# Where transform sets stand between the matmuls of a gated MLP

## The chip, the cores and the metric

The kernel runs on one core of a Trainium2 chip. The time is device microseconds (us) from one launch; lower is better. A core has engines that run side by side, each through its own list of instructions in order: TensorE (PE, matmuls, writes to PSUM), VectorE (DVE), ScalarE (ACT), GpSimd (POOL) and SyncE (SP), which here issues nearly all DMA transfers. They wait for each other by semaphores.

## The reference, cut to what matters

Two blocks are applied to the same layer-normed input, their results are added, and the gradients with respect to nine inputs are computed as well. S = 2048 rows, D = 512 columns, F = 1376 hidden columns, all bfloat16.

```python
xn  = layernorm(x)
kv  = shift_conv(k, shift_k) * v                  # 4 taps along the rows
y   = irfft(rfft(kv, 2S) * rfft(ssm_k, 2S))[:S] + kv * ssm_D
A   = xn * y                                      # long convolution
B   = ((xn @ w_gate) * (xn @ w_up)) @ w_down      # gated MLP
out = x + A + B
# and the vector-Jacobian product of out with grad_out
```

The backward pass needs a second convolution (of grad_out * xn, for dkv) and a third correlation (for d ssm_k), and for the MLP the gradient of its hidden layer, dx and three weight gradients.

## The kernel before, in words

The long convolution is a transform in two steps. `stage1` multiplies each of 16 blocks of rows by a table and stores the result in DRAM (FD), one for each of three signals. Eight groups (`groups`, L710) then do the second step: for group g and signal sg, `g_fwd` (L554) loads a tile X from FD and does sixteen matmuls that use a 64 by 32 part of the array (ps, two PSUM tiles); ScalarE copies both to SP (S1). `g_mul` (L569) multiplies two such spectra on VectorE: two long products T and U (L577), then an addition or subtraction for each half of T (L579, L580). `g_inv` (L583) does sixteen matmuls on T into two PSUM tiles (pg), ScalarE copies them to GO, and SP stores GO in DRAM (GD). Sixteen such matmuls, forward or inverse, are called a **set** here. There are 24 forward and 24 inverse ones. A forward set also issues the load of the X that is four further on (L567).

The MLP goes through eight chunks of 256 rows. `ffn1` (L478) does a chunk in six **pieces** of two hidden blocks (the sixth has one): gate and up (pgu, sixteen matmuls of 256 columns), the gradient of the hidden layer (pdh, eight), copies on ScalarE (gu, dh), products on VectorE (hd), a store of hd (HDD). `yb` (L518) follows one chunk behind: for each of two halves of the rows (sb), y (py, eleven matmuls of 512 columns; VectorE adds x, L529) and dx (px, twenty-two matmuls over two weights; ScalarE copies it, L535).

Both are Python generators. `main` (L748) yields after every piece of `ffn1` and after every y and dx of `yb`. The loop at L770 adds a pace to an account at every such yield and moves a second generator, `side`, one step for every whole number in the account. `side` is first `front` (the normalisation and `stage1`, at 170/71 steps per yield), then `groups`, which sets the pace to GPACE = 0.96. `groups` issues four loads of X, then yields four times with nothing in between, then goes through its sets, one per step (before the first inverse set is one more empty step). So about every piece, y and dx is followed by a set. In what order the instructions stand on each engine in the end is decided by the layer that records them, which has priorities (`high_priority` lifts copies and products) and its own estimates.

PSUM has three tiles of two banks (P2: pgu, ps, pg, later pt, pq, pu) and two of one bank (P1: pdh, py, px, later pd). ps and pg take two of the three.

Behind the stage stands a tail (`dw` and its sides, L911 and L1063): 2048-column transposes of hd out of HDD (tile hb, transposes pt, copies nath and natd), weight gradients (pd, pu), the last transform step (`st1p`, pq, on tiles g1 that are loaded from GD, L793), and elementwise work. Its first loads (hb, g1) are issued behind the last store of GD on SP. These names are used below.

Of the kernel before, what the change touches and what calls it, by code (L numbers as in the profile page):

```python
# [25 lines left out]
NCH = 8  # L26
# [150 lines left out]
def kernel(  # L177
# [42 lines left out]
    def act(o, i):  # L220
        nc.scalar.copy(o, i)  # L221
# [16 lines left out]
    def P2(name, shape, dt=F32):  # L238
        return ps2.tile(shape, dt, name=name, tag="p2")

    def P1(name, shape, dt=F32):
        return ps1.tile(shape, dt, name=name, tag="p1")
# [235 lines left out]
    def ffn1(ch):  # L478
        xt, gt = XT.pop(ch)
        hd = hds[ch % 2]  # L480
        HD[ch] = hd
        for fb0 in range(0, NFB, 2):
            blk = FBLK[fb0:fb0 + 2]
            n = len(blk)
            fw = blk[0][1]
            pgu = P2("pgu", [P, 2, 2, 256])
            pdh = P1("pdh", [P, 2, 256])

            def gate_up():
                for i, (f0, w) in enumerate(blk):  # L490
                    for t, W in enumerate((Wu, Wg)):
                        for c in range(NC4):
                            nc.tensor.matmul(pgu[:w, i, t, :], lhsT=W[:, c, f0:f0 + w], rhs=xt[:, :, c, :],  # L493
                                             start=(c == 0), stop=(c == NC4 - 1))

            def down():
                for i, (f0, w) in enumerate(blk):
                    for c in range(NC4):
                        nc.tensor.matmul(pdh[:w, i, :], lhsT=WdT[:, c, f0:f0 + w], rhs=gt[:, :, c, :],  # L499
                                         start=(c == 0), stop=(c == NC4 - 1))  # L500

            for f in ((gate_up, down) if ch or fb0 else (down, gate_up)):
                f()
            if ch == 0:
                mid(fb0 // 2)
            gu = gup.tile([P, 2, 2, 256], BF, name="gu")
            dh = gup.tile([P, 2, 256], BF, name="dh")
            act(gu[:fw, :n], pgu[:fw, :n])
            act(dh[:fw, :n], pdh[:fw, :n])
            with tc.high_priority(offset=SOON):  # L510
                nc.vector.tensor_tensor(hd[:fw, fb0:fb0 + n, 0, :], gu[:fw, :n, 0, :], gu[:fw, :n, 1, :], op=ALU.mult)  # L511
                nc.vector.tensor_tensor(hd[:fw, fb0:fb0 + n, 1:3, :], gu[:fw, :n],  # L512
                                        dh[:fw, :n].unsqueeze(2).to_broadcast((fw, n, 2, 256)), op=ALU.mult)
            if ch < NCH - 1:
                nc.sync.dma_start(HDD[:, fb0:fb0 + n, ch], hd[:, fb0:fb0 + n])
            yield

    def yb(ch):  # L518
        hd = HD.pop(ch)
        bx = ybo.tile([P, 2, 2, D], BF, name="bx")  # L520
        xb = ybo.tile([P, 2, D], BF, name="xb", bufs=1)
        nc.sync.dma_start(xb[:], x_n[:, 2 * ch:2 * ch + 2, :])
        for sb in range(2):
            ss = slice(sb * 128, (sb + 1) * 128)
            py = P1("py", [P, D])
            for fb, (f0, fw) in enumerate(FBLK):
                nc.tensor.matmul(py[:], lhsT=hd[:fw, fb, 0, ss], rhs=Wd[:fw, fb, :], start=(fb == 0), stop=(fb == NFB - 1))  # L527
            with tc.high_priority(offset=SOON):
                nc.vector.tensor_tensor(bx[:, sb, 0, :], py[:], xb[:, sb, :], op=ALU.add)  # L529
            yield  # L530
            px = P1("px", [P, D])
            for t, W in ((1, WTS[0][:, 0]), (2, WTS[0][:, 1])):
                for fb, (f0, fw) in enumerate(FBLK):
                    nc.tensor.matmul(px[:], lhsT=hd[:fw, fb, t, ss], rhs=W[:fw, fb, :], start=(t == 1 and fb == 0), stop=(t == 2 and fb == NFB - 1))  # L534
            act(bx[:, sb, 1, :], px[:])  # L535
            if sb == 1:
                nc.sync.dma_start(BX[:, 2 * ch:2 * ch + 2, :, :], bx[:])
            yield

# [5 lines left out]
    def g_load(n):  # L547
        g, sg = divmod(n, 3)
        if g < 8:
            X = gpool["x"].tile([P, 4, D], BF, name="X", bufs=4)  # L550
            nc.sync.dma_start(X[:], FD[sg, 16 * g:16 * g + 16].rearrange("k c r d -> (k c r) d").rearrange("(q m) d -> m q d", q=4))
            GX[n] = X

    def g_fwd(g, sg):  # L554
        X = GX.pop(3 * g + sg)
        S1 = gpool["a"].tile([P, 2, 2, D], BF, name="SP", bufs=4)
        for ri in range(2):
            ps = P2("ps", [P, 2, D])
            for q in range(4):
                for a in range(2):  # L560
                    nc.tensor.matmul(ps[32 * q:32 * q + 32, a, :],  # L561
                                     lhsT=TB.EF[64 * a:64 * a + 64, 4 * g + q, ri].rearrange("p k j -> p (k j)"),
                                     rhs=X[64 * a:64 * a + 64, q, :], start=True, stop=True)
            with tc.high_priority(offset=SOON):
                act(S1[:, ri], ps[:])
        GS[sg] = S1
        g_load(3 * g + sg + 4)  # L567
# [37 lines left out]
    def seq(*its):  # L605
        for it in its:
            for _ in it:
                yield
# [40 lines left out]
    def mid(n):  # L649

        if n == 0:
            wd_transposes(*WPARTS[1])
        elif n == 2:
            wd_transposes(*WPARTS[2])
# [55 lines left out]
    def groups():  # L710
        st_es.close()
        gpool["a"] = gpool["es"].enter_context(tc.tile_pool(name="ga", bufs=1, side="right", reuse_waits="tile"))
        gpool["x"] = gpool["es"].enter_context(tc.tile_pool(name="gx", bufs=1, side="right", reuse_waits="tile"))
        for n in (0, 2, 3, 1):
            g_load(n)
        pace[0] = GPACE
        for _ in range(4):
            yield
        g_fwd(0, 0)
        yield  # L720
        g_fwd(0, 2)
        g_mul(1, 0, 2, True)
        yield
        g_fwd(0, 1)
        g_mul(0, 0, 1, False)
        g_mul(2, 1, 2, True)
        yield
        yield
        g_inv(0, 0)
        yield  # L730
        for g in range(1, 9):
            for sg, dg, o, ops in ((0, -1, 1, ()), (1, -1, 2, ((0, 0, 1, False),)),
                                   (2, 0, 0, ((1, 0, 2, True), (2, 1, 2, True)))):
                if g < 8:
                    g_fwd(g, sg)
                    for m in ops:
                        g_mul(*m)
                    yield
                if g + dg < 8:
                    g_inv(g + dg, o)  # L740
                    yield

    GPACE = 0.96
    pace = [170 / 71]
    gpool["es"] = ExitStack()
    side = seq(front(), groups())

    def main():  # L748
        for ch in range(NCH):
            it = ffn1(ch)  # L750
            for n, _ in enumerate(it):
                if ch == 0:
                    tables(n)
                yield
                if n == 1 and 0 < ch < NCH - 1:
                    load_xt(ch + 1)
                if ch == 0 and n == 3:
                    load_xt(1)
                if n == (5 if ch == 1 else 1) and 0 < ch < NCH - 1:
                    while len(WTS) < 2:  # L760
                        next(side)
                    yield from yb(ch - 1)
        yield "wa"
        yield from yb(NCH - 2)
        yield from yb(NCH - 1)

    mainit = main()
    acc = -5 * pace[0]
    mdone = 0
    for tag in mainit:  # L770
        if tag == "wa":
            wa_es.close()
            c1 = ctx.enter_context(tc.tile_pool(name="c1", bufs=1, reuse_waits="tile"))
            xnC = c1.tile([P, R, D], BF, name="xnC")
            goC = c1.tile([P, R, D], BF, name="goC")
            nc.sync.dma_start(goC[:], go_n)
            nc.sync.dma_start(xnC[:], XN[:])
        acc += pace[0]
        while acc >= 1:
            acc -= 1  # L780
            next(side, None)
    for _ in side:
# [319 lines left out]
```

## Time and profile before

| | |
|---|---|
| time, median of 3 runs | 508.24 us (505.66 to 508.82) |
| profiled execution, its own time | 507.66 us |
| its span, first to last instruction | 505.9 us |
| busy: TensorE, VectorE, ScalarE | 479.2, 341.0, 328.7 us |
| mean granted clock of TensorE | 0.996 |
| 131.6 us to 153.2: TensorE busy | 21.50 of 21.60 us |
| 153.2 us to 325.0: TensorE, ScalarE busy | 168.57, 126.67 of 171.80 us |
| 325.0 us to 337.0: TensorE busy | 11.71 of 12.00 us |

The transform sets begin at 137 us and end at 313 us; dx of the last chunk ends at 325 us and the tail begins. In lines of the trace in order of time, the columns are start, length, engine, line, operation, tiles (out<-in), shapes and the number of instructions that are merged into the line; brackets tell how long the engine was idle before it and what ended that. In a list of waits the numbers are the total, the number of times and the longest. "Issue" as what was waited for means that the profile shows nothing.

### The profile page before, as it was taken

The numbers are of one execution on the slowest core, as the hardware profiler recorded it, in microseconds if no ns is written. First come the engines' busy times: TensorE is split into PE (matmuls) and PEld (weight loads), VectorE is DVE, ScalarE is ACT, GpSimd is POOL, SyncE is SP. The second block draws the span as 40 slices with busy tenths as digits, with TensorE's granted clock in tenths as the row PEclk, the third lists the DMA queues.
The fourth block names the chain that finished last, engine by engine and source line by source line (L and its number), as shares of the span: only waits on it lengthen the run. The fifth ranks groups of instructions, "written<-read, shape, count | busy, mean of one in ns | idle before, by whom it ended". The sixth has DMA issues, their size and how long they took to land.

```text
span 505.9 us, 10724 instructions
## 1 busy us (share of the span) xinstructions
PE 479.2 (95%) x4420; PEld 323.4 (64%) x4457; DVE 341.0 (67%) x633; ACT 328.7 (65%) x358; POOL 6.7 (1%) x17
## 2 busy tenths in 40 slices
PE   8789889998999999999999999999999989999996
PEld 7677554645747547547457733566776768777885
DVE  3987998888365748866648956031288987999800
ACT  3676788857837949759569975286575524555551
POOL 3000000000000000000000000020000000000000
PEclk9998999999999999999999999999999999999999
DMA  9999997989896957967968396999999999897513
GB/s 279 375 330 335 292 298 250 341 269 344 299 296 212 278 187 242 289 206 233 271 198 264 127 343 222 374 359 370 375 334 342 371 294 351 269 309 240 166 60 108
DMA packets 98045, 140.41 MB, mean 278 GB/s; under 512 B 18474, under 2 KB 72047, under 8 KB 96108
## 3 DMA queue, kind: packets, MB, share of 16 engines
q1 hardware_dynamic: 96668, 138.94, 83.3%
q10 hardware_dynamic: 1328, 0.79, 0.5%
q8 instruction: 35, 0.57, 0.5%
q14 instruction: 14, 0.11, 0.1%
HBM read 72.76 MB, written 63.41 MB: 269 GB/s over the span
## 4 chain that ended last, share of the span: by engine, by line
PE 55%; DMA 20%; DVE 10%; ACT 9%; issue 3%; SPq 2%; ACTq 0%
PE px L534 12%; PE pgu L493 9%; PE pu L939 8%; PE py L527 6%; PE pdh L499 5%; PE pd L922 4%; DMA FD<-fst 3%; PE pg L590 2%; PE pt L815 2%; PE ps L561 2%; ACT gu L221 2%; DMA out_dram<-o 2%; DMA khC<-in_A_k_dram 2%; DMA bb<-BX 2%; ACT fst L221 2%
## 5 line engine op out<-in xcount | busy, mean ns | idle before, releaser
L939 PE MATMUL pu<-natd,xnC 128*128 128x256 bf16 (+1 forms) x704 | 79.1, 270 | 0.7 <-ACT nath L221 0.7
L534 PE MATMUL px<-WT,hd 128*128 128x512 bf16 (+1 forms) x346 | 78.9, 379 | 0.5 <-issue 0.3
L939 PEld LDWEIGHTS <-xnC 128*128 128x128 bf16 x704 | 67.2, 98 | 8.7 <-issue 1.0
L534 PEld LDWEIGHTS <-hd 128*128 128x128 bf16 (+1 forms) x352 | 33.5, 98 | 42.7 <-issue 3.7
L221 ACT COPY natd<-pt 128x2048 bf16<-128x2048 bf16 (+1 forms) x22 | 40.4, 1838 | 25.4 <-PE pt L815 25.4
L493 PE MATMUL pgu<-xt,Wu 128*128 128x256 bf16 (+1 forms) x352 | 53.3, 274 | 3.5 <-DVE WdT L224 2.0
L493 PE MATMUL pgu<-xt,Wg 128*128 128x256 bf16 (+1 forms) x352 | 52.8, 273 | 0.0
L221 ACT CAST gu<-pgu 128x1024 bf16<-128x1024 f32 (+1 forms) x48 | 45.3, 946 | 11.3 <-PE pgu L493 11.0
L221 ACT CAST GO<-pg 128x1024 bf16<-128x1024 f32 x48 | 46.3, 1019 | 7.7 <-issue 4.8
L577 DVE TENSOR_TENSOR T<-SP 128x2048 bf16<-128x2048 bf16 x24 | 29.3, 1223 | 31.9 <-ACT SP L221 31.9
L499 PE MATMUL pdh<-gt,WdT 128*128 128x256 bf16 (+1 forms) x352 | 47.1, 275 | 1.5 <-DVE WdT L224 1.3
L221 ACT CAST SP<-ps 128x1024 bf16<-128x1024 f32 x48 | 46.6, 1034 | 1.9 <-PE ps L561 1.9
L221 ACT CAST fst<-pf 128x1024 bf16<-128x1024 f32 x40 | 39.2, 1034 | 12.5 <-DMA FD<-fst 10.8
L493 PEld LDWEIGHTS <-Wu 128*128 128x128 bf16 (+1 forms) x352 | 33.0, 100 | 19.9 <-issue 15.1
L527 PE MATMUL py<-Wd,hd 128*128 128x512 bf16 (+1 forms) x166 | 40.5, 380 | 0.8 <-issue 0.5
L499 PEld LDWEIGHTS <-WdT 128*128 128x128 bf16 (+1 forms) x352 | 34.9, 101 | 6.8 <-DVE WdT L224 1.5
L922 PE MATMUL pd<-goC,nath 128*128 128x512 bf16 (+1 forms) x166 | 38.3, 379 | 0.5
L221 ACT CAST bx<-px 128x512 bf16<-128x512 f32 x16 | 9.5, 592 | 45.1 <-PE px L534 45.1
L493 PEld LDWEIGHTS <-Wg 128*128 128x128 bf16 (+1 forms) x352 | 34.9, 100 | 3.6
L511 DVE TENSOR_TENSOR hd<-gu 128x512 bf16<-128x512 bf16 (+1 forms) x48 | 19.1, 398 | 24.3 <-ACT gu L221 24.2
L512 DVE TENSOR_TENSOR hd<-gu,dh 128x1024 bf16<-128x1024 bf16 (+1 forms) x48 | 30.7, 642 | 1.1 <-ACT dh L221 0.2
L527 PEld LDWEIGHTS <-hd 128*128 128x128 bf16 (+1 forms) x176 | 16.3, 98 | 22.8 <-issue 4.8
(155 smaller groups left out, 677.7 us busy)
## 6 DMA issues: line engine op xcount, KB each, us to landing
HDD<-hd SPq DMA_DIRECT2D x35, 384.0 KB, 4.8
hb<-HDD SPq DMA_DIRECT2D x10, 1344.0 KB, 11.4
FD<-fst SPq DMA_DIRECT2D x24, 512.0 KB, 3.9
X<-FD SPq DMA_DIRECT2D x24, 512.0 KB, 5.5
GD<-GO SPq DMA_DIRECT2D x24, 512.0 KB, 3.8
g<-GD SPq DMA_DIRECT2D x8, 1024.0 KB, 8.8
BX<-bx SPq DMA_DIRECT2D x8, 512.0 KB, 3.4
bb<-BX SPq DMA_DIRECT2D x8, 512.0 KB, 7.6
```

The costliest lines, as they stand in the source:

```text
L221: nc.scalar.copy(o, i)
L493: nc.tensor.matmul(pgu[:w, i, t, :], lhsT=W[:, c, f0:f0 + w], rhs=xt[:, :, c, :], start=(c == 0), stop=(c == NC4 - 1))
L499: nc.tensor.matmul(pdh[:w, i, :], lhsT=WdT[:, c, f0:f0 + w], rhs=gt[:, :, c, :], start=(c == 0), stop=(c == NC4 - 1))
L511: nc.vector.tensor_tensor(hd[:fw, fb0:fb0 + n, 0, :], gu[:fw, :n, 0, :], gu[:fw, :n, 1, :], op=ALU.mult)
L512: nc.vector.tensor_tensor(hd[:fw, fb0:fb0 + n, 1:3, :], gu[:fw, :n], dh[:fw, :n].unsqueeze(2).to_broadcast((fw, n, 2, 256)), op=ALU.mult)
L527: nc.tensor.matmul(py[:], lhsT=hd[:fw, fb, 0, ss], rhs=Wd[:fw, fb, :], start=(fb == 0), stop=(fb == NFB - 1))
L534: nc.tensor.matmul(px[:], lhsT=hd[:fw, fb, t, ss], rhs=W[:fw, fb, :], start=(t == 1 and fb == 0), stop=(t == 2 and fb == NFB - 1))
L561: nc.tensor.matmul(ps[32 * q:32 * q + 32, a, :], lhsT=TB.EF[64 * a:64 * a + 64, 4 * g + q, ri].rearrange("p k j -> p (k j)"), rhs=X[64 * a ...
L577: tt(W[:].rearrange("p c a d -> p c (a d)"), A[:, i:i + 1].rearrange("p c a d -> p c (a d)").to_broadcast((P, 2, 2 * D)), B[:].rearrange(" ...
L590: nc.tensor.matmul(pg[q // 2][64 * a:64 * a + 64, q % 2, :], lhsT=TB.EI[32 * q:32 * q + 32, 2 * g + a, yi].rearrange("p k c -> p (k c)"), ...
L922: nc.tensor.matmul(pd[:fw, :], lhsT=nt[:, r, :fw], rhs=goC[:, r, :], start=(r == 0), stop=(r == R - 1))
L939: nc.tensor.matmul(pu[:, c, :, :fw], lhsT=xnC[:, r, cs(c)], rhs=ng[:, :, r, :fw], start=(r == 0), stop=(r == R - 1))
```

## The change

The pace is replaced by named places as soon as `groups` has begun. Each yield of `main` now carries a value; where it is true, `side` moves one step. It is true behind every y and every dx, behind the first half of every dx (a new yield between the two weights, `"half"`), and behind the first, third and fifth piece of a chunk; in the last chunk behind all pieces but the sixth. While `front` runs the pace is as it was, and `"half"` doesn't count. The four empty steps at the start of `groups` become one.

```diff
 def ffn1(ch):
-            yield
+            yield fb0 in (0, 4, 8) or (ch == NCH - 1 and n > 1)
 def yb(ch):
                 nc.vector.tensor_tensor(bx[:, sb, 0, :], py[:], xb[:, sb, :], op=ALU.add)
-            yield
+            yield True
             px = P1("px", [P, D])
             for t, W in ((1, WTS[0][:, 0]), (2, WTS[0][:, 1])):
                 for fb, (f0, fw) in enumerate(FBLK):
                     nc.tensor.matmul(px[:], lhsT=hd[:fw, fb, t, ss], rhs=W[:fw, fb, :], start=(t == 1 and fb == 0), stop=(t == 2 and fb == NFB - 1))
+                if t == 1:
+                    yield "half"
             act(bx[:, sb, 1, :], px[:])
...
-            yield
+            yield True
 def groups():
         for n in (0, 2, 3, 1):
             g_load(n)
-        pace[0] = GPACE
-        for _ in range(4):
-            yield
+        pace[0] = None
+        yield
         g_fwd(0, 0)
...
-    GPACE = 0.96
 def main():
-            for n, _ in enumerate(it):
+            for n, set_here in enumerate(it):
...
-                yield
+                yield set_here
...
-        acc += pace[0]
-        while acc >= 1:
+        if pace[0] is None:
+            if tag and tag != "wa":
+                next(side, None)
+            continue
+        if tag != "half":
+            acc += pace[0]
+        while acc >= 1 and pace[0]:
             acc -= 1
             next(side, None)
```

A chunk's pieces and its `yb` thus hold nine places (three and six) where the pace gave 9.6 steps (5.76 and 3.84). The built program has the same instructions as before in another order. On TensorE the order is the same up to the first transform set and, but for a matmul here and there, from the first pu on.

## The prediction, made before the run

> **What bounds the kernel now.** I read the page's busy shares first, then TensorE's list of waits in the stage that changes (137 us, the first transform matmul, to 325 us, the last matmul of dx), then the same stretch in order of time.
>
> ```profile
> PE 479.2 (95%) x4420; PEld 323.4 (64%) x4457; DVE 341.0 (67%) x633; ACT 328.7 (65%) x358; POOL 6.7 (1%) x17
> ```
>
> TensorE is the bound. Its waits between 137 and 325 us (total, times, longest):
>
> ```profile
> PE ps L561 <- ACT GO L221: 1.5, 4, 0.7
> PE py L527 <- issue: 0.5, 3, 0.2
> PE pg L590 <- ACT SP L221: 0.5, 2, 0.2
> PE px L534 <- issue: 0.3, 2, 0.2
> ```
>
> The two "issue" rows are no waits: in each such place the first matmul of the chain has no record (x10 or x21 where the code has 11 or 22). What is left is 2.0 us of 188, all of it TensorE waiting for ScalarE to empty a PSUM buffer, where a set follows the sixth MLP piece of a chunk. By the distance of its starts (281.34 to 284.62) ScalarE needs 0.93 + 0.48 us for a piece (gu, dh) and 1.87 for a set, 3.28; TensorE needs 2.61 for the piece (pgu at 131.63 to the next at 134.24) and 0.67 for the set, also 3.28. From 260 to 293 us ScalarE is busy 32.97 of 33.00 us. So **no more than 2.0 us can be gained in the stage itself**, and all else depends on its two ends, where now TensorE does not wait:
>
> ```profile
> 142.43 1.23 DVE L577 TENSOR_TENSOR T<-SP 128x2048 bf16<-128x2048 bf16 x1 [1.64 <-ACT SP L221]
> ...
> 147.96 1.22 DVE L577 TENSOR_TENSOR T<-SP 128x2048 bf16<-128x2048 bf16 x1 [1.84 <-ACT SP L221]
> 149.11 1.22 DVE L577 TENSOR_TENSOR U<-SP 128x2048 bf16<-128x2048 bf16 x1
> 150.24 0.68 DVE L529 TENSOR_TENSOR bx<-py,xb 128x512 bf16<-128x512 f32 x1
> 150.84 0.68 DVE L579 TENSOR_TENSOR T<-T,U 128x1024 bf16<-128x1024 bf16 x1
> 151.44 0.68 DVE L580 TENSOR_TENSOR T<-T,U 128x1024 bf16<-128x1024 bf16 x1
> ```
>
> The first product ready for an inverse set is done at 152.1; the set starts at 153.20, 1.1 us later. The other end:
>
> ```profile
> 312.53 0.64 PE L590 MATMUL pg<-T,EI 32*64 32x512 bf16 x16
> 315.65 0.46 SPq L799 DMA_DIRECT2D hb<-HDD  x1
> 316.21 1.63 SPq L793 DMA_DIRECT2D g<-GD  x2
> 325.00 0.94 PE L815 MATMUL pt<-ident,hb 128*128 128x128 bf16 x14
> 325.89 1.89 PE L837 MATMUL pq<-g,IW 128*128 128x512 bf16 x8
> 326.10 1.86 ACT L221 COPY nath<-pt 128x2048 bf16<-128x2048 bf16 x1 [0.31 <-PE pt L815]
> 336.94 3.76 PE L939 MATMUL pu<-natd,xnC 128*128 128x256 bf16 x33
> ```
>
> The last set ends at 313.1; its copies free SP at 315.6, SP then issues the loads of hb (6.9 us to landing, at 322.5) and g (8.9 and 9.9, at about 325.1 and 326.6), and dx and y of the last chunk (11.9 us) cover both.
>
> **The change part by part.** No engine gets or loses work; the built order has 49 entries into a group of transform matmuls before and 49 after (28 of them behind an MLP piece before, 17 after). An entry costs TensorE about 0.10 us wherever it stands (pdh at 155.53 to ps at 156.50: 0.97 for eight matmuls at 0.109; px at 183.61 to ps at 188.47: 4.86 for 22 at 0.217). So the move itself is worth nothing, and splitting px for a set costs nothing more.
>
> 1. *Sets beside y and half dx.* A set every 11 matmuls of 0.217 us plus 0.67 is one in 3.05 us, against 1.9 us of ScalarE (and 0.58 for bx twice a chunk); in the MLP a set on every second piece is 3.28 + 1.41 = 4.7 us of ScalarE against 5.9 of TensorE. I followed the three PSUM buffers through a chunk by hand with these durations and found no wait. On SP each set's X load and GD store move with it; they change places with neighbouring stores and with the two transposing loads of a chunk (3.2 and 4.0 us of SP's time). An X lands in 5.5 us and is used four forward sets after its issue, some 24 us in the densest part; a GO buffer comes round after three inverse sets, 18 us there, against 3.8 us for its store. That cover is ample. **-2.0 us**; if ScalarE's start is late (chunk 7 keeps sets on five pieces in a row) -1.0.
>
> 2. *One empty step in place of four at the start.* The first forward set stands one MLP piece earlier, so it is reached at 134.24 instead of 136.96. Its X was issued at 129.85 and took 4.8 us: 134.65. With the 0.05 until TensorE starts: **+0.45** (0 to 1.85, had it taken the 6.2 us of the next but one). The second forward set then comes after the same work as before, at 140.45 (before 139.99). The third comes after half of dx, 143.5, not all of it plus a wait (145.41); its X is the one that waits for the last FD write, issued at 137.3, and lands by 143.5 at 6.2 us: nothing.
>
> 3. *The first inverse set.* VectorE's chain starts 0.46 later than in the rows above, at 142.9, runs the first product to 146.5 and then, in the built order, T, U, one more T of the third product (1.14 apart), the add that makes half of the second product's T (done 150.6), bx, the other add (done 151.8). TensorE has after the third set half of dx, y, three matmuls of dx: it is at the first eight matmuls of the inverse set at 149.6 and waits to 150.65, is at the second eight at 151.25 and waits to 151.85. **+1.65** (0.9 if the T of the third product slips behind, 2.6 if bx and that T both delay it). The cover that hid this, half of dx more, is what the change takes away.
>
> 4. *The last products.* Behind the last forward set (at k) ScalarE and VectorE need as before 2.56 us until the first T starts, then 1.14 + 1.14 + 1.14 to the add: half of T at k + 6.65, all at k + 7.25. The inverse set that reads it was 8.5 us behind (301.01 to 309.48); now two half-chains are in between, 0.57 + 2.38 + 0.10 twice, k + 6.1. Waits 0.55 and 0.35: **+0.9** (0 to 1.6). The last product is done at k + 10.3 and its second eight matmuls are due at k + 10.4: nothing.
>
> 5. *The junction.* Behind the last set now stand half of dx, y, dx: 44 matmuls, 9.6 us, not 55. hb is issued 2.55 us after the set's end and lands after 6.9, at 9.45: just in time (up to +1 if it takes longer). g lands 2.4 to 3.4 us after the end of dx (call it P). The built order has taken this into account: behind the first 16 transposes comes one matmul of pd, which needs their copy (nath, 1.86 us), and only then pq. In before pq filled that gap. So TensorE waits from P + 1.05 to P + 3.05; then pq to 5.0, two groups of transposes to 7.1, 15 of pd to 10.4, pq to 12.2, transposes; ScalarE copies yC from 4.3 to 6.25, natd twice to 9.95, od, dd to 13.25, and the PSUM buffer of that dd is the one for pu: pu at P + 14.2, before P + 11.95: **+2.25** (lower end +0.7: the later wait of 1.55 us of pk for khC, at the end of a chain through SP and VectorE, may swallow 1.55). And SP now has the store of the last bx, which waits for the end of dx, ahead of the second g load: issued at P + 1.2, not 8 us before P; at 8.9 to 11.0 us it lands at P + 10.1 to 12.2, for a pq due at P + 10.4: **+0.7** (0 to 1.8). Behind it on SP hb, v and k loads start 0.5 us later.
>
> Behind that the order of the tail is the same, and TensorE is 95% busy there, so nothing gives the delay back.
>
> **Sum:** 0.45 + 1.65 - 2.0 + 0.9 + 2.25 + 0.7 = +3.95. The profiled execution took 507.66 us (span 505.9), 0.58 below the median 508.24: 507.66 + 3.95 = **511.6 us**. Lower ends together: 0 + 0.9 - 2.0 + 0 + 0.7 + 0 = -0.4, 507.3; upper ends: 1.85 + 2.6 - 1.0 + 1.6 + 2.25 + 1.8 + 1 = +10.1, 517.8.
>
> **Rivals.**
> *ScalarE's relief alone counts.* Place: the sixth piece of each chunk, price -2.0 us: 505.7. It decides once the two ends together cost under 2.0 us: it needs VectorE's first and last chain 1 us faster each, and g early enough that the scheduled pd matmul is the only wait, given back at khC. For it: the chain that ended last runs from the end of dx through SP's loads, VectorE and khC to pk, and TensorE has slack of 1.55 there. Against: that chain itself starts with the same products and copies. Chance 0.25, 504.5 to 509.
>
> *Loads at the junction take the busy time.* hb loads elsewhere take 10.5 us in the median and up to 11.9, the third g took 11.0. If hb takes 10.5 now that 2.4 us of cover is gone: +3.6 in front of everything, with the rest 515.2; the second g at 11 adds 1. Chance 0.2, 513.5 to 518.
>
> *It does not do what it says.* The recording layer still orders by its own estimates: it put three matmuls of dx before the first inverse set and split that. Elsewhere the built order has the sets where named. If the sets' places do not matter to any wait: 507.7. Chance 0.05.
>
> *TensorE's clock.* Granted clock is 1.00 in the changed stage and 0.99 over the first 131.6 us, where TensorE's longest wait is 2.2: 1.3 us is all that a start from rest has cost. The waits above are at most 2.0 each; if one of them grew and lost the clock, +1.3: 512.9. Chance 0.02, inside the forecast's range. The Trainium skill (TensorE: Matmul & The Clock Gate, Part 1: The HAM clock gate) puts the loss of clock behind an idle window of about 3.4 us; by it these waits lose none. The trace agrees so far: waits up to 0.70 in the stage, clock 1.00.
>
> **Chances.** Forecast (+2 to +6 us, 509.7 to 513.7) 0.48, relief 0.25, slow loads 0.2, no effect 0.05, clock 0.02. 1% is 5.1 us, about what a measurement tells from no change, so 503.2 to 513.3 is "within". Forecast but its top, relief, no effect: 0.66; slower by more: 0.31; faster by more would need more than the 2.0 us that exist: 0.03. Range 506 to 516.
>
> **What would show it.** Right: TensorE's waits for ScalarE's GO and SP in the stage go to about 0; a wait of 1 to 2.6 us of the first pg for T around 150 us, one of about 1 us around the last group, pd waiting about 2 us for nath at the end of dx, pu starting 14 us behind it. Wrong: pg without a wait for T, hb landing clearly after dx ends, or pq waiting for g by 2 us and more; a shift that comes from the MLP chunks in between would mean that I misjudged ScalarE.

## The result, and the profile after

| | before | after |
|---|---|---|
| time, median (13 runs each) | 507.23 us (505.53 to 508.82) | 509.64 us (508.42 to 512.16) |
| profiled execution, its own time | 507.66 us | 509.33 us |
| its span | 505.9 us | 507.5 us |
| mean granted clock of TensorE in it | 0.996 | 0.992 |

The ratio of the times is **1.0061, with a 95% interval of 1.0043 to 1.008**: some 3.1 us slower (2.2 to 4.1), inside 1%. The forecast was +3.95 us and the range 506 to 516.

To place the loss, both traces are cut at three matmuls that stand at the same point of the work: the first pgu of chunk 2 (call it A; the order of TensorE is the same up to there), the first pt of the tail (P, the end of dx) and the first pu of the tail.

| us | start to A | A to P | P to pu | pu to end |
|---|---|---|---|---|
| before | 131.63 | 193.37 | 11.94 | 168.96 |
| after | 132.02 | 192.93 | 15.18 | 167.37 |
| difference | +0.39 | -0.44 | +3.24 | -1.59 |

The first column is no effect of the change: the point A lies between 131.1 and 133.9 us in all the traces of this study, with the same order in front of it. The second column, the stage that the change is about, comes out 0.4 us shorter; the third, twelve microseconds at the end of dx, loses 3.2. These two executions are only 1.6 us apart, because the last column gives 1.59 back; item 5 below says what is known of it.

The busy shares of the kernel after:

```profile
PE 482.7 (95%) x4457; PEld 323.4 (64%) x4457; DVE 341.2 (67%) x633; ACT 330.8 (65%) x358; POOL 6.8 (1%) x17
```

TensorE is still the bound. It is "busy" 3.5 us longer with the same matmuls. Part of that is records (4457 of 4457 here, 4420 before), part is real and is shown at the end of this section.

TensorE's waits of the kernel after between 137 and 330 us (total, times, longest):

```profile
PE pd L928 <- ACT nath L221: 2.0, 1, 2.0
PE pg L592 <- DVE T L581: 1.5, 2, 1.0
PE pg L592 <- DVE T L582: 0.6, 2, 0.5
```

The waits for ScalarE's GO and SP (2.0 us before) are gone. In their place TensorE waits for VectorE's T at the first inverse set and at the last but one, and for ScalarE's nath. The same in order of time:

```profile
135.11 0.62 PE L563 MATMUL ps<-X,EF 64*32 64x512 bf16 x16 [0.31 <-DMA X<-FD]
...
150.96 0.42 PE L592 MATMUL pg<-T,EI 32*64 32x512 bf16 x8 [1.02 <-DVE T L581]
152.16 0.42 PE L592 MATMUL pg<-T,EI 32*64 32x512 bf16 x8 [0.45 <-DVE T L582]
...
311.42 0.42 PE L592 MATMUL pg<-T,EI 32*64 32x512 bf16 x8 [0.48 <-DVE T L581]
312.02 0.42 PE L592 MATMUL pg<-T,EI 32*64 32x512 bf16 x8 [0.18 <-DVE T L582]
317.98 0.46 SPq L805 DMA_DIRECT2D hb<-HDD  x1
324.95 0.94 PE L821 MATMUL pt<-ident,hb 128*128 128x128 bf16 x14
326.04 1.87 ACT L221 COPY nath<-pt 128x2048 bf16<-128x2048 bf16 x1 [0.31 <-PE pt L821]
327.96 0.39 PE L928 MATMUL pd<-goC,nath 128*128 128x512 bf16 x1 [1.96 <-ACT nath L221]
328.19 3.36 PE L843 MATMUL pq<-g,IW 128*128 128x512 bf16 x8
```

hb, issued at 317.98, has landed after 6.9 us, just before dx ends: the first pt at 324.95 waits for nothing. pd stands behind the transposes and waits 1.96 us for their copy. The last line is the one that nobody had foreseen: the eight matmuls of pq take 3.36 us, against 1.89 in the trace of before. The windows of the kernel after around it (the stretch, busy us and count of TensorE, its weight loads, VectorE, ScalarE and GpSimd, then the granted clock, the DMA share and GB/s):

```profile
325.00:328.00 3.00, 1.04 (x18) 0.87 (x18) 0.00 (x0) 2.45 (x2) 0.00 (x0) 1.00 1.00 381
328.00:329.00 1.00, 1.00 (x4) 0.42 (x5) 0.00 (x0) 0.00 (x0) 0.00 (x0) 0.72 0.75 258
329.00:330.00 1.00, 1.00 (x3) 0.30 (x2) 0.00 (x0) 0.08 (x1) 0.79 (x1) 0.50 0.88 295
```

From 328.45 to 331.86 us TensorE has half of its clock. That the matmuls run at half speed there counts as busy time, so no list of waits shows it. It is worth 1.7 us: half of 3.41, or 1.47 in pq and 0.26 in the fourteen transposes behind it (1.20 us, where the others take 0.94). So by these rows about half of the 3.24 us from P to pu is the clock; the other half is the wait of pd, 1.96 us in place of one of 0.23 in before (together an estimate of 3.4).

### The profile page after: what moved, and what is told of

It is laid out like the page before. It is cut to its first block, busy times and chain, and to the rows that moved or that the text cites. A ratio compares the mean times of both kernels' runs of the same rounds, so it can differ in the third digit from the quotient of the medians.

```text
span 507.5 us, 10754 instructions
## 1 busy us (share of the span) xinstructions
PE 482.7 (95%) x4457; PEld 323.4 (64%) x4457; DVE 341.2 (67%) x633; ACT 330.8 (65%) x358; POOL 6.8 (1%) x17
## 4 chain that ended last, share of the span: by engine, by line
PE 74%; DMA 9%; DVE 8%; ACT 6%; issue 2%; SPq 0%; ACTq 0%
PE pu L945 14%; PE pgu L493 13%; PE px L534 11%; PE pd L928 7%; PE pdh L499 6%; PE py L527 5%; PE pt L821 5%; DMA FD<-fst 3%; PE pq L843 3%; PE pg L592 3%; PE ps L563 2%; DMA x_b<-in_A_q_dram 2%; PE pf L347 2%; ACT nath L221 1%; PE pk L967 1%
## 5 line engine op out<-in xcount | busy, mean ns | idle before, releaser
L534 PE MATMUL px<-WT,hd 128*128 128x512 bf16 (+1 forms) x352 | 82.0, 380 | 0.0
L534 PEld LDWEIGHTS <-hd 128*128 128x128 bf16 (+1 forms) x352 | 32.5, 98 | 44.6 <-issue 8.9
L221 ACT CAST GO<-pg 128x1024 bf16<-128x1024 f32 x48 | 46.3, 1015 | 20.9 <-PE pg L592 13.5
L221 ACT COPY natd<-pt 128x2048 bf16<-128x2048 bf16 (+1 forms) x22 | 40.2, 1834 | 22.8 <-PE pt L821 22.7
L928 PE MATMUL pd<-goC,nath 128*128 128x512 bf16 (+1 forms) x176 | 40.1, 379 | 2.0 <-ACT nath L221 2.0
L527 PE MATMUL py<-Wd,hd 128*128 128x512 bf16 (+1 forms) x176 | 41.6, 379 | 0.0
L821 PEld LDWEIGHTS <-hb 128*128 128x128 bf16 (+1 forms) x462 | 27.6, 98 | 4.6 <-issue 1.7
L821 PE MATMUL pt<-ident,hb 128*128 128x128 bf16 (+1 forms) x462 | 30.4, 219 | 0.1
```

The costliest lines, as they stand in the source:

```text
L821: nc.tensor.transpose(pt[:, r, :fw], hs[:, (r % 2) * 128:(r % 2) * 128 + 128], ident[:fw, :fw])
L928: nc.tensor.matmul(pd[:fw, :], lhsT=nt[:, r, :fw], rhs=goC[:, r, :], start=(r == 0), stop=(r == R - 1))
```

## The experiments: the two ends

By these rows the start of the stage costs 1.5 to 2 us (the first inverse set stands where its product is not ready) and the junction at the end of dx some 3 (TensorE arrives where a copy is not ready), and the places in the middle gain. If that is so, mending the two ends leaves a kernel faster than before; if the places themselves cost time, it does not. Two edits mend one end each and leave all the rest.

**e1_swap** lets the first inverse set take the second product, which is ready earlier, and the next inverse set the first one's turn.

```diff
-        g_inv(0, 0)
+        g_inv(0, 1)
...
-                    g_inv(g + dg, o)
+                    g_inv(g + dg, 0 if (g, sg) == (1, 0) else o)
```

> The changed kernel, but the first inverse set is that of the product which VectorE finishes first (signal 1 in place of 0; the two change places). Theory: TensorE's two waits for T near 150 us (1.02 and 0.45 us in the trace of the changed kernel, 1.8 us with the split of px) are lost time. Then: no wait of pg for T before 300 us, and 1.8 us less than the changed kernel, ratio to the kernel before about 1.0025. Rival: the time comes back elsewhere (ScalarE or X late behind the set): waits move, ratio stays 1.006.

**e2_early** adds one place in chunk 5, so that all later sets stand one place earlier and 55 matmuls, not 44, stand behind the last.

```diff
-            yield fb0 in (0, 4, 8) or (ch == NCH - 1 and n > 1)
+            yield fb0 in ((0, 2, 4, 8) if ch == 5 else (0, 4, 8)) or (ch == NCH - 1 and n > 1)
```

> The changed kernel with one place more in chunk 5 (behind the second piece), so that every later set stands one place earlier and 55 matmuls of y and dx follow the last set, not 44. Theory: pd does not wait for nath, granted clock stays 1.00 behind the end of dx, pu starts 12 us behind it and not 15.2; of these 3.2 us the wait of pk for khC takes 1.55 back: 1.7 us less than the changed kernel, ratio about 1.003. Rival (loads at the junction are slow whatever the cover): pq or pt wait for g or hb, pu still 14 us or more behind the end of dx.

**e3_swap_early** has both edits, and **e4_swap_early2** has both, with the fourth place in chunk 4 as well (`ch in (4, 5)`).

> Both edits together: 3.5 us less than the changed kernel, ratio 0.999 (0.9955 by the profiled spans alone: the stage's 3.5 us won against 0.4 for X and 0.85 for the last products). If the waits hide behind each other the sum is smaller: ratio 1.002 or more.

> As the run before it, with one place more in chunk 4 as well, 66 matmuls behind the last set. Theory: the cover of 55 was enough, so the same within 0.2%. Rival: more cover lets hb and g land earlier and the chain through SP to khC start earlier: the wait of pk for khC shrinks and up to 1.5 us more is won.

| | ratio to before | median | A to P | P to pu | pu to end |
|---|---|---|---|---|---|
| before, beside these four | 1 | 507.69 us | 193.37 | 11.94 | 168.96 |
| e1_swap | 1.0040 [1.0015, 1.0065] | 509.64 us | 191.62 | 16.03 | 167.86 |
| e2_early | 0.9975 [0.9956, 0.9993] | 507.08 us | 192.56 | 11.95 | 168.40 |
| e3_swap_early | **0.9954 [0.9935, 0.9973]** | 505.40 us | 191.42 | 11.94 | 168.03 |
| e4_swap_early2 | 0.9953 [0.9933, 0.9973] | 505.65 us | 191.35 | 13.17 | 166.36 |

(The stretches of before are those of its one trace.) The four ran on one chip and can be compared with each other. The swap is worth 1.7 us between e2 and e3; the earlier last set is worth 4.2 us between e1 and e3, 4.1 of them from P to pu (0.66 of it a wait for the second hb, which the trace of e1_swap has and that of the kernel after has not). Together they turn a loss of 0.6% into a gain of 0.46%. So the places themselves cost nothing: with both ends mended they are faster than the pace by about 2.3 us, and e3_swap_early and e4_swap_early2 beat both kernels. e1_swap alone, expected at 1.0025, can't be told from the kernel after by its interval; that the swap is worth something rests on e2 against e3. e2_early and e3_swap_early came out some 0.5% and 0.4% under the ratios expected of them (1.003 and 0.999; 0.9955 was named for e3 as what the profiled spans alone give, and that is what came): the junction was worth more than I had put on it. A fourth place in chunk 4 too adds nothing that can be measured.

In order of time, e1_swap at the first inverse set:

```profile
149.79 0.64 PE L592 MATMUL pg<-T,EI 32*64 32x512 bf16 x16
```

Sixteen matmuls in one piece with no wait, where the kernel after has two pieces, 1.02 and 0.45 us late. And e3_swap_early at the end of dx:

```profile
323.93 0.95 PE L821 MATMUL pt<-ident,hb 128*128 128x128 bf16 x14
...
324.82 1.89 PE L843 MATMUL pq<-g,IW 128*128 128x512 bf16 x8
326.94 0.94 PE L821 MATMUL pt<-ident,hb 128*128 128x128 bf16 x14 [0.23 <-ACT nath L221]
```

With the last set one place earlier the recording layer has put pq right behind the first transposes, as in before; pq fills the time of the copy, and pd comes later. In e1_swap, whose end is that of the kernel after, pd waits and pq is slow again:

```profile
326.94 0.39 PE L928 MATMUL pd<-goC,nath 128*128 128x512 bf16 x1 [1.96 <-ACT nath L221]
327.16 3.51 PE L843 MATMUL pq<-g,IW 128*128 128x512 bf16 x8
```

## The experiments: the clock

Theory: TensorE loses half of its clock for some 3.4 us because it stands idle for about 2 us in front of pd. Rival: the clock falls at times of its own, and one of those fell on pq by chance. The experiments put work that nobody reads into that gap and leave everything else; what they add, they add inside time that TensorE would wait. **e5_fill_mm** puts eight matmuls of 512 columns behind the first 16 transposes of the tail, **e6_fill_tr** 26 transposes, **e9_fill2** and **e10_fill4** two and four of the matmuls. The diff is that of e5_fill_mm.

```diff
             hid_t(0, t)
+            if t == 0:
+                pw = P1("fill", [P, 2, 256])
+                for i in range(8):
+                    nc.tensor.matmul(pw[:], lhsT=ident[:], rhs=hbs[0][:, i % 7, 0:2, :], start=True, stop=True)
```

> The changed kernel with eight matmuls of 512 columns into an unused PSUM tile between the first transposes of the tail and the matmul of pd that waits for nath (1.73 us of TensorE in a gap of 1.96; their result is read by nobody). Theory: in the changed kernel TensorE's clock drops to half behind this gap, which costs 1.5 us; with work in the gap it stays at 1.00 there. Then pq takes 1.9 us and not 3.4, pu starts 13.7 us behind the end of dx and not 15.2, mean granted clock over the runs 0.996 as in the kernel before and not 0.992, time 1.5 us less than the changed kernel, ratio 1.003. Rival: the drop has another cause (DMA, chance): clock and time stay as in the changed kernel.

> The same with 26 transposes of 128 columns (1.7 us) in the gap in place of the matmuls. If transposes count as work for the clock: as with the matmuls. If they do not (the first sixteen of the tail did not help either): clock drops, mean granted clock 0.992, ratio 1.006.

> The changed kernel with two matmuls of 512 columns (0.217 us each, their result is read by nobody) behind the first 16 transposes of the tail: the gap in front of the first pd shrinks from 1.96 to about 1.5 us; its end, and what stands behind it, stay in place. Theory 1 (TensorE loses half of its clock behind a gap of about 2 us and not behind shorter ones; 1.02 us around 151 us did not cost it): pq takes 1.89 us, mean clock 0.9955, ratio about 1.003. Theory 2 (any gap clearly over 1.0 us at this place costs the clock): pq takes about 3.4 us, mean clock 0.993, ratio 1.006.

> As the one with two matmuls, with four: the gap shrinks to about 1.1 us. Both theories expect pq in 1.89 us here, a mean clock of 0.9955 and a ratio of about 1.003; pq in about 3.4 us would mean that it is not the length of the gap that counts.

| | wait of pd | pq | mean clock, all runs | wait of pt for hb at P | later waits of pk for kd | ratio to before |
|---|---|---|---|---|---|---|
| after | 1.96 | 3.36 | 0.9929 (13 runs) | 0 | 0 | 1.0061 [1.0043, 1.008] |
| e1_swap | 1.96 | 3.51 | 0.9930 (10) | 0 | 0 | 1.0040 [1.0015, 1.0065] |
| e9_fill2 | 1.74 in its row, 1.52 in truth (below) | 1.89 | 0.9950 (5) | 0 | 1.51 | 1.0051 [1.0033, 1.0069] |
| e10_fill4 | 1.09 | 1.89 | 0.9942 (5) | 1.27 | 0.76 | 1.0069 [1.0045, 1.0093] |
| e6_fill_tr | 0.51 | 1.89 | 0.9952 (10) | 0.62 | 0.37 | 1.0031 [1.0012, 1.0049] |
| e5_fill_mm | 0.23 | 1.89 | 0.9956 (10) | 0.67 | 0.24 | 1.0029 [1.0008, 1.0049] |

The same place in e5_fill_mm, e6_fill_tr and e9_fill2, in order of time:

```profile
327.41 1.89 PE L924 MATMUL fill<-hb,ident 128*128 128x512 bf16 x7
329.54 0.39 PE L932 MATMUL pd<-goC,nath 128*128 128x512 bf16 x1 [0.23 <-ACT nath L221]
329.76 1.89 PE L843 MATMUL pq<-g,IW 128*128 128x512 bf16 x8
```

```profile
328.22 1.61 PE L924 MATMUL fill<-ident,hb 128*128 128x128 bf16 x26
330.34 0.39 PE L932 MATMUL pd<-goC,nath 128*128 128x512 bf16 x1 [0.51 <-ACT nath L221]
330.56 1.89 PE L843 MATMUL pq<-g,IW 128*128 128x512 bf16 x7
```

```profile
328.74 0.39 PE L932 MATMUL pd<-goC,nath 128*128 128x512 bf16 x1 [1.74 <-ACT nath L221]
328.96 1.89 PE L843 MATMUL pq<-g,IW 128*128 128x512 bf16 x8
```

In all four pq is back at 1.89 us. The row of e9_fill2 shows a wait that is too long: its trace holds the weight loads of both added matmuls but the record of one only. With the second, 0.22 us behind the first, the wait is 1.52 us, as was expected. The mean clock over all runs agrees: 0.993 in the two kernels that have the gap of 1.96 us, 0.9954 over the 20 runs of e5_fill_mm and e6_fill_tr, and 0.9957 over 35 runs of before. Single runs spread from 0.985 to 1.000, so the five runs each of e9_fill2 and e10_fill4 don't tell by their means. One stretch of 3.41 us at half clock is 0.0034 of the mean. So the gap in front of pd is what takes the clock here, by the means in most executions (an estimate: 0.0025 of 0.0034).

The length of the gap alone does not decide it. In all twelve traces TensorE also waits 1.95 us until about 22.5 us; in five of them the clock falls behind that wait (at 22.8 to 23.5 us), in the seven others, before and after among them, it stays. What differs is in part where the wait falls. In every trace that has more than one, the slow stretches start whole multiples of 3.413 us apart: in the kernel after at 38.32, 328.45 and 505.94 us (85 and 52 steps), in e7_nohalf at 23.22, 40.29 and 142.69 (5 and 30). So in these traces the clock falls only at fixed times, and it matters how a gap lies between two of them. In the step before the loss at pq TensorE is busy 0.43 of the time in the kernel after (1.45 of 3.41 us, 325.04 to 328.45) and 0.41 in e1_swap. At the same place the least busy step has 0.55 in e9_fill2 (with the missing matmul), 0.61 in e10_fill4, 0.74 in e6_fill_tr and 0.79 in e5_fill_mm, and the clock stays. The busy share is no sharp limit either: before loses the clock behind a step of 0.60 (34.47 to 37.88 us), and e2_early keeps it behind one of 0.43 (20.46 to 23.87). What else counts stays open.

What the fill is worth in time is less clear. e5_fill_mm (1.003 expected) and e6_fill_tr came out 0.3% (1.6 us) better than the kernel after; e9_fill2 and e10_fill4, for which 1.003 was expected, did not, and **that expectation failed**. One trace of each shows where the gain may have stayed: the one of e9_fill2 waits 1.51 us at the second pk of the tail, for a product on VectorE, and 0.69 for hb before pu; that of e10_fill4 1.27 for hb at P and 0.76 at pk.

So the lost clock is shown as 1.7 us at its place, and its worth at the end of the kernel is left open between nothing and 1.6 us: in these traces other waits of the tail, on loads and on VectorE, are longer by part of it.

## The experiments: the middle of the stage

In the traces the stage gained more than the 2.0 us that I had called its most. Two explanations: halving dx spreads the sets better than the idle rows tell, or a wait costs more than its idle row shows. **e7_nohalf** (the swap in it too) takes the half of dx away and puts the sets behind five of six pieces, none behind the sixth, up to chunk 4, and behind all pieces from there on. **e8_row** (the kernel after otherwise) puts them behind the fourth, fifth and sixth piece, three in a row, as the pace has them around the sixth.

The first diff is that of e7_nohalf, the second that of e8_row:

```diff
-            yield fb0 in (0, 4, 8) or (ch == NCH - 1 and n > 1)
+            yield fb0 < 10 or ch >= 5
...
-                if t == 1:
-                    yield "half"
```

```diff
-            yield fb0 in (0, 4, 8) or (ch == NCH - 1 and n > 1)
+            yield fb0 in (6, 8, 10) or (ch == NCH - 1 and n > 1)
```

> The kernel of the third run (signal 1 first, 55 matmuls behind the last set) without the halving of dx: sets behind y, dx and the first five pieces of a chunk, behind the sixth in the last three chunks alone. Theory A (what counts is that ScalarE gets a pause once a chunk): only the three sixth pieces cost, 0.65 us each, 2 us more than the third run, ratio 0.9995; the last products have more distance, 0.7 us less: 0.998. Theory B (the halves of dx are worth it by themselves, sets beside matmuls of 512 columns being cheaper): waits in every chunk, ratio 1.003 or more.

> The changed kernel with the three sets of a chunk's MLP behind its fourth, fifth and sixth piece, in a row. Theory: ScalarE has a copy of a set to do behind every piece and then the short sixth, so TensorE loses time at the sixth piece as in the kernel before: piece, set and what comes behind take 0.3 to 0.65 us more than the 1.98 us of their matmuls. If three in a row are still free, the loss needs a longer run of sets.

The measure is the period of one chunk, from the first matmul of a y (or dx) to that of the next chunk's. In before, with ten sets in it, and in the kernel after, with nine:

```profile
172.32 2.32 PE L527 MATMUL py<-Wd,hd 128*128 128x512 bf16 x10 [0.16 <-issue]
...
208.29 2.32 PE L527 MATMUL py<-Wd,hd 128*128 128x512 bf16 x10 [0.16 <-issue]
```

```profile
174.18 2.54 PE L527 MATMUL py<-Wd,hd 128*128 128x512 bf16 x11
...
208.88 2.54 PE L527 MATMUL py<-Wd,hd 128*128 128x512 bf16 x11
```

| | period | sets in it | less 0.67 for a tenth set | recorded waits in it |
|---|---|---|---|---|
| before | 208.29 - 172.32 = 35.97 | 10 | 35.30 | 0.28 |
| after | 208.88 - 174.18 = 34.70 | 9 | 34.70 | 0 |
| e7_nohalf | 213.57 - 178.87 = 34.70 | 9 | 34.70 | 0 |
| e8_row | 216.77 - 181.48 = 35.29 | 9 | 35.29 | 0.28 |

(In before, e7_nohalf and e8_row the first matmul of the chain has no record at either end, so the difference holds.) The next chunk repeats it: 35.98 us in before, 34.69 in the kernel after, 34.70 in e7_nohalf, 35.34 in e8_row. e7_nohalf has the period of the kernel after without any half of dx: **issuing dx in two halves is worth nothing by itself**. What counts is that no set follows the sixth piece. e8_row brings the wait back, one in a chunk, and its cost lies where it was expected (0.3 to 0.65 us):

```profile
204.06 0.41 PE L563 MATMUL ps<-X,EF 64*32 64x512 bf16 x8
204.75 0.41 PE L563 MATMUL ps<-X,EF 64*32 64x512 bf16 x8 [0.28 <-ACT GO L221]
205.22 0.60 PE L493 MATMUL pgu<-xt,Wu 128*128 128x256 bf16 x4
```

The row says 0.28 us; the period says 0.59, as much as in before (0.60). A set without a wait, in the kernel after:

```profile
170.99 0.63 PE L563 MATMUL ps<-X,EF 64*32 64x512 bf16 x16
171.55 0.61 PE L493 MATMUL pgu<-xt,Wu 128*128 128x256 bf16 x4
```

From the set's start to the next matmul it takes 0.56 us there and 1.16 in e8_row: the wait costs 0.60. The records explain most of the rest. Eight matmuls of a set end 0.41 after they began though each is recorded as 0.38 long, so they lie nearly on top of each other, and sixteen end after 0.63, so the second eight begin about 0.22 behind the first. In e8_row they begin 0.69 behind it, 0.47 late; idle time is counted only from the recorded end at 0.41, so 0.19 of this is in no row. The remaining 0.13 lies between the second eight and the next pgu (0.47 us there, 0.34 in the kernel after) and stays unexplained.

e7_nohalf as a whole came out at 1.0015 [0.9994, 1.0035] (509.07 us). Its interval reaches from 0.9995, expected if only the sixth pieces count, to 1.003, expected if the halves count by themselves, so the time doesn't decide between them; the periods do. It is not better than e3_swap_early, and its trace shows a reason at the start: my edit also put the second forward set ahead of all but one matmul of y, where its X is still under way, and the clock went again behind that wait (a window of its trace below, columns as above):

```profile
142.63 1.05 PE L561 MATMUL ps<-X,EF 64*32 64x512 bf16 x16 [2.39 <-DMA X<-FD]
```

```profile
142.60:146.00 3.40, 3.04 (x21) 1.04 (x23) 0.73 (x1) 1.93 (x2) 0.00 (x0) 0.51 1.02 356
```

e8_row has a single run, of 510.61 us, and no interval; only its rows are used.

## Why the prediction was right, and where it was not

The forecast of +3.95 us held (+3.1 by the ratio, 2.2 to 4.1), with the right sign and the two places named. Some terms of the sum were off in both directions, and that they balanced is luck in part: the stage gained more than forecast and the second g cost nothing, while 1.7 us of lost clock, which is not in the sum, came on top.

1. *Sets beside y and half dx*, forecast -2.0. The waits for GO and SP vanished, as said, and no X and no PSUM buffer was late in the middle. The **size was wrong**: the wait measured by the periods is worth 0.6; if all six of before (four for GO, two for SP) are, that is -3.6. "No more than 2.0 us can be gained in the stage itself" read the idle rows as if they were the cost. The sums agree: A to P is -0.44 with 2.4 us of new recorded waits in it (items 2 to 4), so the rest gained at least 2.9.
2. *One empty step in place of four*, forecast +0.45: the wait for X is 0.31 in the kernel after, 0.62 and 0.65 in e1_swap and e3_swap_early. Right.
3. *The first inverse set*, forecast +1.65: 1.02 + 0.45 recorded, and 1.84 by the position of the matmuls behind it (152.51 - 149.13, less 0.65 for three of dx, 0.67 for the set and 0.22 for one more of dx). Right; e1_swap, which takes the wait away, is 1.3 us shorter from A to P, and the swap is worth 1.7 between e2 and e3.
4. *The last products*, forecast +0.9 (0.55 and 0.35): 0.48 and 0.18. Right, a little high.
5. *The junction.* The wait of pd for nath, forecast at 2.0 us, is 1.96. hb "just in time": it was, with 6.9 us, in the kernel after; in other traces with the same order pt waited 0.6 to 1.3 for it, inside the bound of +1 or a little over. The second g, forecast +0.7, cost nothing: pq stood at P + 11.67 and found its data, with no wait recorded. The load that can be late there is the second hb, issued behind g: 0.65 to 0.69 in e1_swap, e5_fill_mm and e9_fill2, nothing in the kernel after. pu came at P + 15.18, not 14.2: the clock. Without its 1.7 us pu would stand at P + 13.5 (an estimate from these rows), so the step of +2.25 for pd was itself some 0.7 too high. The lower end, that khC's wait of 1.55 swallows the delay, looks as if it had come true: the wait is gone, and the tail is 1.59 shorter. But it is gone in e2_early and e3_swap_early too, where nothing is late at the junction, and their tails take 168.0 to 168.4. So that wait of before isn't a counterweight to this delay; why it is in the one trace of before stays open.

*The rivals.* That ScalarE's relief alone counts (505.7, chance 0.25) was wrong for this kernel, but e3_swap_early is what it described: both ends mended, 505.4 us. The slow loads (0.2) did not come in the kernel after. That the change does nothing (0.05) is out: each of its places is seen in the waits.

*TensorE's clock* (0.02) was the **step that failed**. I had its size nearly right (+1.3; it was 1.7), and had the wait of 2.0 us in front of pd; but I gave it a chance only "if one of them grew". The granted clock of 0.99 over the first 131.6 us, which I took for a start from rest, was already such a loss: in the trace of before the clock is 0.50 from 37.88 to 41.30 us, and the only wait of more than 0.9 us in the 15 us ahead of it is one of 1.12. The traces show the clock going behind 1.96 us in two kernels, behind 2.39 in a third and behind 1.95 around 22 us in five traces of twelve; it did not go behind 1.02 at 151 us. The Trainium skill (TensorE: Matmul & The Clock Gate, Part 1: The HAM clock gate) puts the loss behind an idle window of about 3.4 us, and by it none of these waits should have cost anything; here the measurement differs and decides. What agrees with that section is the length of the loss: 3.41 us at half clock in each of these traces, against its figure of about 3.4.

## What to carry to other kernels

Moving work to better places in the middle of a stage is paid for at its two ends: look at what the last moved piece covers (here a copy of 1.9 us and two loads of 7 to 10) and leave as much work behind it as before, then the gain is kept. A wait's idle row is not its cost where short matmuls overlap; compare the period of a loop instead, and take into account that a gap of 2 us can cost a slow stretch of the clock, 1.7 us here. When the recorded order puts an operation ahead of the one that used to fill its wait, the order itself is the first thing to look at (this is argued: e2_early changed the order and the cover of the loads together).

## What was not expected of the hardware

- TensorE's granted clock fell to 0.5 for 3.41 us, 0.5 us after a gap of 1.96 us had ended (gap 326.0 to 327.96, loss 328.45 to 331.86), at a time that lies a whole multiple of 3.413 us from the other losses of the same trace. All traces of this study but two (e4_swap_early2, e10_fill4) have one to three such stretches ahead of the very end, most in the first 130 us at changing places (23, 38 to 40, 66, 126 to 128 us); they make up part of the 2.8 us by which the point A moves.
- 26 transposes in the gap kept the clock at 1.00 as eight matmuls did (mean 0.9952 and 0.9956 over ten runs each); in the step from 326.73 to 330.14 us of e6_fill_tr TensorE does transposes alone, 2.52 us of 3.41. The Trainium skill (TensorE: Matmul & The Clock Gate, Part 4: PE-mode transpose) says of the transposes that they don't count as work in the same way; this run doesn't bear that out.
- A wait inside a set of 64 by 32 matmuls cost 0.59 us where the row shows 0.28.
